# FFT convolution with two gated layers: the transform's last stores, fetches and a decoded weight piece in another order

## The chip, the cores and the metric

One core of a Trainium2 chip runs the whole program. The time is device time in microseconds (us), the median of three runs. Engines: TensorE (PE) multiplies matrices, VectorE (DVE), ScalarE (ACT) and GpSimd (POOL) work on elements, SyncE (SP) issues the transfers. DMA moves data between memory and the core.

## The reference

A circular convolution along the sequence by FFT, then two gated layers on 6016 tokens of 256 channels, all in float32:

```python
X = np.fft.rfft(x, axis=1)                      # x: 2 x 3008 x 256
Y = X * (filt_r + 1j * filt_i)[None, :, :]
x = np.fft.irfft(Y, n=3008, axis=1).reshape(6016, 256)
g = x @ w_gate                                  # 256 x 1536
x = (g / (1 + np.exp(-g)) * (x @ w_val)) @ w_out
h = x @ w_in                                    # 256 x 2048
return (h * np.clip(h + 3.0, 0.0, 6.0) / 6.0) @ w_out2
```

## The kernel before, in words

**Transform.** 3008 = 47 x 64, so the FFT is two stages of small matrix products. Sixteen steps k handle one slice of 32 channels of one batch each, batch 0 and 1 in turns of four, first the lower 128 channels (a = 0), then the upper (a = 1). A step's work is spread over the loop's turns: `over_n1(k)` (L415) and `over_n2(k)` (L431) on TensorE, `filter_product(k)` on VectorE (L444) and GpSimd (`us`, four operations), `back(k)` (L457) two turns later on TensorE, whose result ScalarE copies into `turned` (L462). `store` (L466) writes `turned` to memory, and a fetch (L526) reads it in another arrangement, since the last stage of the inverse needs the 47-part axis across partitions: `to_time` (L158) does that last stage for one block of up to 512 tokens. A batch has six blocks. Blocks 0 and 1 of batch 0 are made at the transform's end by `form`; all others inside the layers, fetched by `load_g` (L140).

**Precision.** Each operand is split in a high part (rounded, ScalarE: L116 for x, L486 and L487 for weights) and the low rest (VectorE or GpSimd subtracts: L109). `l1` makes a product of three: high by high, and each high by the other's low.

**Weights.** They come as 64-bit numbers and are decoded on the core, 128 columns of each matrix a piece f, by six steps on VectorE behind one on ScalarE: `start` (L187, ScalarE), `leading` = L196, L198, L201, `rest` = L204, L206, L112. Then come `high_w1` (ScalarE) and `low_w1` (VectorE or GpSimd). Two halves of a buffer (`x`) hold the pieces in turn, so piece f + 2 is loaded (`load_dec`, L479) when piece f is done with the half.

**Layers.** The first loop's turn t does one piece of one block: 12 matmuls L236 for gate and value, ScalarE's Silu (L613), VectorE's product (L622). The first 24 turns alternate between blocks 0 and 1, two turns each (p = t // 2), so that pieces are needed half as fast: f = 0 and 1 at t = 0 to 3, f = 2 at t = 4. After two turns of a block the hidden values are split into `hs` (ScalarE L116, VectorE L109), and after the following two turns of l1 TensorE takes them into the output product, 12 matmuls L121. This stage, where pieces are decoded beside the layers, runs to about 165 us.

**What sets the order.** Everything is written out by hand: each engine works its queue in the order in which the code emits. `at` and `send` put decode steps and transfers at turns k of the transform; `lead`, `rest` and `part` (L615) put `start` and `leading`, `rest`, and `high_w1` with `low_w1` at turns t of the layers. SyncE issues transfers in order, and a transfer that must wait holds up those behind it.

Of the kernel before, what the change touches and what calls it, by code (L numbers as in the profile page):

```python
# [9 lines left out]
F32 = mybir.dt.float32  # L10
# [6 lines left out]
P = 128  # L17
B, S, D = 2, 3008, 256
N1, N2 = 47, 64
N1P = 48  # L20
# [3 lines left out]
F1, F2 = DFF1 // P, DFF2 // P  # L24

BLOCKS = [(8 * j, min(8, N1 - 8 * j)) for j in range(6)]
# [52 lines left out]
def fft_conv_glu_mlp(ctx: ExitStack, tc: tile.TileContext, x, filt, mats, sgn, w1, w2, out):  # L79
    nc = tc.nc  # L80
# [4 lines left out]
    work = ctx.enter_context(tc.tile_pool(name="work", bufs=2))  # L85
# [39 lines left out]
    def rows(i, n=64):  # L125

        return slice(i * 64, i * 64 + n)

    def new_g():
        return work.tile([P, 7 * D], F32, tag="g", name="g", bufs=1)  # L130

    def turns(j, n):

        return 32 * j // N1, -(-(32 * j + n // 2) // N1)
# [9 lines left out]
    def new_xs():  # L144
        return work.tile([P, 2, 2, 512], F32R, tag="xs", name="xs")
# [85 lines left out]

    def l1(acc, w, xs, n):

        for r, v in ((0, 0), (0, 1), (1, 0)):
            for k in range(2):
                nc.tensor.matmul(acc[:, :n], w[:, r, k * P:(k + 1) * P], xs[:, v, k, :n],  # L236
                                 start=(r, v, k) == (0, 0, 0), stop=(r, k) == (1, 1))

    def l2(acc, w, hidden, first, last):
        hs, nt = hidden.hs, hidden.nt  # L240
# [72 lines left out]
    def new_y():  # L313
        return work.tile([P, 1024], F32, tag="y", name="y", bufs=1)
# [37 lines left out]
    with tc.manual_schedule():  # L352
# [10 lines left out]
        N = 16  # L363
# [132 lines left out]
        def at(k, step, *a):  # L496
            todo.setdefault(k, []).append(lambda: step(*a))

        def send(k, *a):
            moves.setdefault(k, []).append(a)  # L500

        moves = {}
        for k in range(1, 13):
            send(k, load_x, k + 3)
        for k, f in ((1, 0), (8, 1), (11, 2)):
            send(k, load_dec, f, 3)
        for j in range(4, 8):
            send(j - 2, load_filter, j)
        for i in range(8):
            send((5, 5, 6, 6, 7, 7, 8, 8)[i], store, 0, 0, i)  # L510
            send((9, 9, 10, 10, 11, 11, 12, 12)[i], store, 1, 0, i)
            send(13, store, 0, 1, i)

        for f, steps in ((0, (4, 5, 5, 6, 7, 8, 9, 10, 10)), (1, (10, 11, 11, 12, 12, 13, 14, 15, 17)), (2, (15, 15, 15, 17))):
            at(steps[0], lambda f: dec[f].start(), f)
            for i in range(len(steps[1:7])):
                at(steps[1 + i], lambda f, i: dec[f].part(i, nc.vector), f, i)
            if f < 2:
                at(steps[7], high_w1, f)
                at(steps[8], low_w1, f)  # L520

        def load_half(j, a, g):
            t0, t1 = turns(*BLOCKS[j][:1], BLOCKS[j][1] * N2)
            g = g[:, :7 * P].rearrange("p (t c) -> p t c", c=P)
            for r in range(2):
                nc.sync.dma_start(out=g[rows(r, N1P), :t1 - t0],  # L526
                                  in_=d2[0].rearrange("q (h n) c -> (q h) n c", h=2)[:, 32 * r + t0:32 * r + t1, a * P:(a + 1) * P])
            return g

        def form(j):  # L530
            xsd[j] = new_xs()
            acc = to_time(gt[j], j, "a")
            for r in range(2):
                split(*time_halves(xsd[j], acc, j, r))

# [3 lines left out]
        for k in range(N + 2):  # L539
            if 1 < k < N:  # L540
                over_n1(k)
            if k >= 2:
                back(k - 2)
            for step, *a in moves.get(k, ()):
                step(*a)
            if k == 12:
                g0 = new_g()
                gt[0] = [load_half(0, 0, g0)]
                gt[1] = [load_half(1, 0, new_y())]
            elif k == N - 1:  # L550
                gt[0].append(load_half(0, 1, g0[:, 7 * P:]))
                gt[1].append(load_half(1, 1, turned[:, 0].rearrange("p q c -> p (q c)")))
            if k < N:
                over_n2(k)
                filter_product(k)
            else:
                form(k - N)
            if k < 3 or 3 < k < 8:
                prepare_filter(k + (k < 3))
            for step in todo.get(k, ()):  # L560
                step()
        load_dec(3)

        n_pair = n_block * G1
        steps = [(s % 2, s // 2) for s in range(2 * G1)] + [divmod(s, G1) for s in range(2 * G1, n_pair)]
# [4 lines left out]
        for t in range(2 * n_pair):  # L572
            p, i = divmod(t, 2)
# [15 lines left out]
            if after:  # L589
                xsd[after] = new_xs()  # L590
                both_halves = to_time(gt[after], blocks[after][1])
            if i == 1 and p >= 1:
                kq, gq = steps[p - 1]
                if gq == 0:
                    accs[kq] = [bank("a") for _ in range(4 if kq > 1 else 2)]
                (l2 if kq > 1 else l2_plain)(accs[kq], wo1[:, gq], hid.pop(p - 1), gq == 0, gq == G1 - 1)
# [15 lines left out]
            h = hid[p].chunk(i)  # L612
            nc.scalar.activation(out=h, in_=hid[p].halves(gate), func=AF.Silu)  # L613

            lead, rest, part = ([f_ for f_ in range(2, F1) if t == 2 * f_ + d] for d in (-5, -4, -3))  # L615
            for f_ in part:
                high_w1(f_)
            for f_ in lead:
# [3 lines left out]
            nc.vector.tensor_tensor(out=h, in0=h, in1=hid[p].halves(val), op=ALU.mult)  # L622
            if i == 0 and p > plain:
                hid[p - 1].low()
            for f_ in part:
                low_w1(f_, nc.gpsimd)
                if f_ + 2 < F1:
                    load_dec(f_ + 2)
# [198 lines left out]
```

## Time and profile before

| | |
|---|---|
| median of 3 runs | 1187.62 us (1186.98 to 1189.38) |
| the profiled execution | 1187.92 us |
| its span, first to last instruction | 1186.1 us |
| TensorE clock granted (mean) | 0.998 |
| PE busy | 1167.2 us, 98% of the span |
| DVE busy | 1012.2 us, 85% |
| ACT busy | 612.8 us, 52% |
| POOL busy | 147.2 us, 12% |

TensorE fills nearly the whole span, so what counts is where it waits. The transform takes the first 78 us, and the places of interest lie between 60 and 170 us.

### The profile page before, as it was taken

To read this page: it belongs to the slowest core of one execution; us is meant where nothing else is said; L and a number is where in the kernel's file an instruction comes from. 1 tells how busy PE (TensorE), PEld (TensorE's weight loads), DVE (VectorE), ACT (ScalarE), POOL (GpSimd) and SP (SyncE) were. 2 spreads that over 40 slices of the span, in tenths; PEclk is the share of its full clock that TensorE was granted. 3 is DMA by queue.
4 is the path that set the end of the run, shared out by engine and by line. 5 is a ranking of instruction groups with operands and counts; after the bars stand their busy time and mean duration, and the time that the engine had idled before them with its cause. 6 is when DMAs were issued, how large, how long until landed. Compare 5 with 4: busy or idle time off the path is not lost.

```text
span 1186.1 us, 21856 instructions
## 1 busy us (share of the span) xinstructions
PE 1167.2 (98%) x9036; PEld 1022.9 (86%) x9036; DVE 1012.2 (85%) x1573; ACT 612.8 (52%) x928; POOL 147.2 (12%) x153
## 2 busy tenths in 40 slices
PE   9899999999999999999999999999999999999997
PEld 7677778888899888888889988998999999898997
DVE  5878896666678888778888899999999999999997
ACT  4553434433344444444445556666566666656654
POOL 4642310000002222022113300000000000000000
PEclk9999999999999999999999999999999999999999
DMA  8963501100113230221112201011001101100100
GB/s 292 290 168 102 147 1 57 24 20 24 31 54 87 83 94 34 87 60 54 39 32 99 80 16 36 1 37 36 18 18 36 34 1 36 36 17 20 34 19 17
DMA packets 43301, 70.33 MB, mean 59 GB/s; under 512 B 3712, under 2 KB 25088, under 8 KB 43200
## 3 DMA queue, kind: packets, MB, share of 16 engines
q1 hardware_dynamic: 42656, 68.40, 18.8%
q8 instruction: 71, 1.16, 0.4%
q10 hardware_dynamic: 544, 0.52, 0.1%
q14 instruction: 30, 0.25, 0.1%
HBM read 46.62 MB, written 22.28 MB: 58 GB/s over the span
## 4 chain that ended last, share of the span: by engine, by line
PE 95%; DVE 2%; DMA 1%; issue 1%; ACT 1%; SPq 0%; POOL 0%; ACTq 0%; DVEq 0%
PE gv L236 54%; PE a L245 32%; PE a L121 3%; PE gv L457 1%; PE gv L158 1%; PE a L431 1%; PE gv L415 1%; DVE hs L109 1%; DVE h L109 0%; DMA xin<-x_in 0%; DVE h L758 0%; SPq L466 0%; DMA d<-turned 0%; DMA g<-d 0%; PE a L158 0%
## 5 line engine op out<-in xcount | busy, mean ns | idle before, releaser
L245 PEld LDWEIGHTS a<-hs,wall 128*128 128x128 f32 x3276 | 408.3, 189 | 14.1 <-issue 1.2
L245 PE MATMUL a<-hs,wall 128*128 128x256 f32 (+1 forms) x3276 | 414.2, 282 | 1.8 <-issue 0.8
L236 PE MATMUL gv<-xs,wall 128*128 128x512 f32 (+1 forms) x1728 | 406.0, 390 | 0.0
L236 PEld LDWEIGHTS gv<-xs,wall 128*128 128x128 f32 x1728 | 320.8, 188 | 64.4
L109 DVE TENSOR_TENSOR hs<-h,hs 128x768 fp32r<-128x768 f32 (+2 forms) x324 | 349.5, 1079 | 21.9 <-ACT hs L292 16.8
L236 PE MATMUL gv<-xs,wi 128*128 128x512 f32 (+1 forms) x1152 | 276.0, 388 | 0.0
L236 PEld LDWEIGHTS gv<-xs,wi 128*128 128x128 f32 x1152 | 210.0, 188 | 37.1 <-DVE xs L109 0.4
L303 ACT CAST hs<-h 128x1024 fp32r<-128x1024 f32 (+1 forms) x156 | 160.8, 1031 | 114.6 <-DVE h L109 114.4
L292 ACT CAST hs<-h 128x768 fp32r<-128x768 f32 (+1 forms) x156 | 128.1, 821 | 151.0 <-PE a L245 102.4
L109 DVE TENSOR_TENSOR h<-h 128x512 f32<-128x512 f32 (+3 forms) x312 | 185.2, 593 | 6.8
L757 ACT ACTIVATE h<-gv 128x512 f32<-128x512 f32 (+1 forms) x192 | 110.0, 590 | 70.8 <-PE gv L236 54.0
L622 DVE TENSOR_TENSOR h<-h,gv 128x512 f32<-128x512 f32 (+1 forms) x144 | 96.7, 672 | 58.1 <-PE gv L236 56.8
L758 DVE SCALAR_TENSOR_TENSOR h<-h,gv 128x512 f32<-128x512 f32 (+1 forms) x192 | 128.7, 670 | 16.0 <-ACT h L757 11.1
L613 ACT ACTIVATE h<-gv 128x512 f32<-128x512 f32 (+1 forms) x144 | 84.8, 589 | 88.0 <-PE gv L236 87.6
L112 DVE TENSOR_TENSOR h<-h 128x256 f32<-128x256 f32 (+1 forms) x156 | 67.5, 432 | 2.1
L112 POOL TENSOR_TENSOR ww<-ww,wa 128x512 f32<-128x512 f32 x16 | 20.8, 1298 | 373.2 <-PE a L245 191.1
L121 PE MATMUL a<-hs,wall 128*128 128x512 f32 x144 | 36.5, 402 | 2.4 <-DVE hs L109 2.4
L121 PEld LDWEIGHTS a<-hs,wall 128*128 128x128 f32 x144 | 26.3, 188 | 12.2 <-DVE hs L109 6.8
L457 PE MATMUL gv<-us,mat 64*64 64x384 f32 x256 | 28.9, 490 | 3.5 <-issue 3.4
L109 POOL TENSOR_TENSOR wall<-x,wall 128x512 fp32r<-128x512 f32 (+1 forms) x20 | 22.9, 1168 | 68.5 <-ACT wall L486 68.5
L109 POOL TENSOR_TENSOR us<-us 128x192 f32<-128x192 f32 x32 | 25.9, 809 | 27.9 <-DVE us L444 23.0
L422 ACT COPY first<-gv 128x384 f32<-128x384 f32 x30 | 14.5, 482 | 26.0 <-PE gv L415 26.0
(83 smaller groups left out, 622.6 us busy)
## 6 DMA issues: line engine op xcount, KB each, us to landing
raw<-w_in SPq DMA_DIRECT2D x16, 512.0 KB, 4.4
xin<-x_in SPq DMA_DIRECT2D x30, 256.0 KB, 5.4
x<-w_in SPq DMA_DIRECT2D x9, 768.0 KB, 4.7
d<-turned SPq DMA_DIRECT2D x32, 192.0 KB, 5.0
yd<-y SPq DMA_DIRECT2D x10, 512.0 KB, 2.9
g<-yd SPq DMA_DIRECT2D x10, 512.0 KB, 3.8
y_out<-y SPq DMA_DIRECT2D x20, 256.0 KB, 2.4
wt<-wd SPq DMA_DIRECT2D x8, 448.0 KB, 3.4
```

What stands on the lines that cost most here:

```text
L109: (engine or nc.vector).tensor_tensor(out=out, in0=a, in1=b, op=ALU.subtract)
L112: (engine or nc.vector).tensor_tensor(out=out, in0=a, in1=b, op=ALU.add)
L121: nc.tensor.matmul(acc, w, v, start=first and i == 0, stop=last and i == 2)
L236: nc.tensor.matmul(acc[:, :n], w[:, r, k * P:(k + 1) * P], xs[:, v, k, :n], start=(r, v, k) == (0, 0, 0), stop=(r, k) == (1, 1))
L245: nc.tensor.matmul(acc[b][:, 256 * h:256 * h + nt], w[:, r, iw], hs[:, v, ih, :nt], start=first and h == 0 and v == 0 and r == 1, stop=las ...
L292: nc.scalar.copy(out=self.parts(0, 0, 3), in_=v(1, 4))
L303: nc.scalar.copy(out=self.parts(0, 3, 7), in_=self.values(4, 8))
L457: nc.tensor.matmul(accs[r][rows(h), :2 * COLS].rearrange("p (o n) -> p o n", o=2), mat[rows(r), w:w + N2], u[rows(r), :, part], start=m == ...
L613: nc.scalar.activation(out=h, in_=hid[p].halves(gate), func=AF.Silu)
L622: nc.vector.tensor_tensor(out=h, in0=h, in1=hid[p].halves(val), op=ALU.mult)
L757: nc.scalar.activation(out=h, in_=pre, func=AF.Relu, bias=3.0)
L758: nc.vector.scalar_tensor_tensor(out=h, in0=h, scalar=6.0, in1=pre, op0=ALU.min, op1=ALU.mult)
```

## The change

`l1` takes its three products in another order: high by high, then the weights' low part by x's high, then the weights' high by x's low. Blocks 0 and 1 are fetched in one piece for each half of the channels, instead of one for each block: `load_lower` at k = 11, `load_upper` at k = 13. The last stores of batch 0 are cut by rows instead of by frequencies: the first 11 rows of each of four groups of 32, which the two blocks read, go ahead of `load_upper`, and the other 21 behind it. Block 0 is formed at k = 16 as before; block 1's last inverse stage is emitted in the layers' turn t = 0 behind that turn's 12 matmuls, and its split behind that turn's product. Piece 2 is loaded at k = 14 (before: 11), and its decoding stands wholly in the layers: `start` and `leading` at t = 0, `rest` at t = 1, `high_w1` and `low_w1` at t = 2. Piece 1's steps stand one to a turn.

```diff
-        for r, v in ((0, 0), (0, 1), (1, 0)):
+        for r, v in ((0, 0), (1, 0), (0, 1)):
             for k in range(2):
                 nc.tensor.matmul(acc[:, :n], w[:, r, k * P:(k + 1) * P], xs[:, v, k, :n],
-                                 start=(r, v, k) == (0, 0, 0), stop=(r, k) == (1, 1))
+                                 start=(r, v, k) == (0, 0, 0), stop=(v, k) == (1, 1))
...
-        for k, f in ((1, 0), (8, 1), (11, 2)):
+        for k, f in ((1, 0), (8, 1), (14, 2)):
             send(k, load_dec, f, 3)
...
-            send(13, store, 0, 1, i)
-
-        for f, steps in ((0, (4, 5, 5, 6, 7, 8, 9, 10, 10)), (1, (10, 11, 11, 12, 12, 13, 14, 15, 17)), (2, (15, 15, 15, 17))):
+
+        for f, steps in ((0, (3, 4, 5, 6, 7, 8, 9, 10, 10)), (1, (10, 11, 12, 13, 14, 15, 16, 16, 17))):
             at(steps[0], lambda f: dec[f].start(), f)
-            for i in range(len(steps[1:7])):
+            for i in range(6):
                 at(steps[1 + i], lambda f, i: dec[f].part(i, nc.vector), f, i)
-            if f < 2:
-                at(steps[7], high_w1, f)
-                at(steps[8], low_w1, f)
-
-        def load_half(j, a, g):
-            t0, t1 = turns(*BLOCKS[j][:1], BLOCKS[j][1] * N2)
-            g = g[:, :7 * P].rearrange("p (t c) -> p t c", c=P)
+            at(steps[7], high_w1, f)
+            at(steps[8], low_w1, f)
+
+        t_end = turns(BLOCKS[1][0], BLOCKS[1][1] * N2)[1]
+
+        def load_lower():
+            g = new_g()[:, :t_end * P].rearrange("p (t c) -> p t c", c=P)
             for r in range(2):
-                nc.sync.dma_start(out=g[rows(r, N1P), :t1 - t0],
-                                  in_=d2[0].rearrange("q (h n) c -> (q h) n c", h=2)[:, 32 * r + t0:32 * r + t1, a * P:(a + 1) * P])
+                nc.sync.dma_start(out=g[rows(r, N1P)],
+                                  in_=d2[0].rearrange("q (h n) c -> (q h) n c", h=2)[:, 32 * r:32 * r + t_end, :P])
             return g
 
+        def store_rows(lo, hi):
+            for h in range(2):
+                for r in range(2):
+                    n = slice(64 * h + 32 * r + lo, 64 * h + 32 * r + hi)
+                    nc.sync.dma_start(out=d2[0][:, n, P:].rearrange("q p c -> p q c"), in_=turned[n, 0])
+
+        def load_upper():
+            g = work.tile([P, t_end * P], F32, tag="xs", name="upper").rearrange("p (t c) -> p t c", c=P)
...
         def form(j):
+            t0 = turns(BLOCKS[j][0], BLOCKS[j][1] * N2)[0]
+            acc = to_time([g[:, t0:] for g in halves], j, "a")
             xsd[j] = new_xs()
-            acc = to_time(gt[j], j, "a")
+            return acc
+
+        def form_end(j, acc):
             for r in range(2):
                 split(*time_halves(xsd[j], acc, j, r))
 
...
-            if k == 12:
-                g0 = new_g()
-                gt[0] = [load_half(0, 0, g0)]
-                gt[1] = [load_half(1, 0, new_y())]
-            elif k == N - 1:
-                gt[0].append(load_half(0, 1, g0[:, 7 * P:]))
-                gt[1].append(load_half(1, 1, turned[:, 0].rearrange("p q c -> p (q c)")))
+            if k == 11:
+                halves = [load_lower()]
+            elif k == 13:
+                store_rows(0, t_end)
+                halves.append(load_upper())
+                store_rows(t_end, 32)
             if k < N:
                 over_n2(k)
                 filter_product(k)
-            else:
-                form(k - N)
+            elif k == N:
+                form_end(0, form(0))
...
+            if t == 0:
+                acc1 = form(1)
...
-            lead, rest, part = ([f_ for f_ in range(2, F1) if t == 2 * f_ + d] for d in (-5, -4, -3))
+            lead, rest, part = ([f_ for f_ in range(2, F1) if t == max(2 * f_ - 5, 0) + d] for d in range(3))
...
+            if t == 0:
+                form_end(1, acc1)
```

TensorE's queue from the last `back` to the layers' first matmuls, before (L158 is block 1, its lower channels in `y`, its upper in `turned`; L236 the layers):

```order
L457 MATMUL gv<-us,mat 64x384 x8
L158 MATMUL a<-mat,y 64x26 x4
L158 MATMUL a<-mat,y 64x47 x16
L158 MATMUL a<-mat,y 64x42 x4
L158 MATMUL a<-mat,turned 64x26 x4
L158 MATMUL a<-mat,turned 64x47 x16
L158 MATMUL a<-mat,turned 64x42 x4
L236 MATMUL gv<-xs,wall 128x512 x48
```

And the same place in the change:

```order
L457 MATMUL gv<-us,mat 64x384 x8
L236 MATMUL gv<-xs,wall 128x512 x12
L158 MATMUL a<-mat,g 64x26 x4
L158 MATMUL a<-mat,g 64x47 x16
L158 MATMUL a<-mat,g 64x42 x4
L158 MATMUL a<-mat,upper 64x26 x4
L158 MATMUL a<-mat,upper 64x47 x16
L158 MATMUL a<-mat,upper 64x42 x4
L236 MATMUL gv<-xs,wall 128x512 x36
```

Block 1's 48 matmuls moved behind the layers' first twelve; `g` and `upper` are the new fetches.

VectorE's queue from the last filter product (L444) on, before (L109 `xs` splits blocks 0 and 1, two operations each; L109 `wall` is piece 1's low part; L112, L196 to L206 decode pieces 1 and 2 in `x`):

```order
L112 TENSOR_TENSOR x_101<-x_101 128x768
L444 TENSOR_TENSOR us<-a,side 128x384 x4
L196 TENSOR_SCALAR x_101<-x_101 128x768
L198 TENSOR_SCALAR x_101<-x_101 128x768
L109 TENSOR_TENSOR xs<-a,xs 128x2x256 x4
L109 TENSOR_TENSOR wall<-x_101,wall 128x512
L109 TENSOR_TENSOR wall<-x_101,wall 128x256
L201 SCALAR_TENSOR_TENSOR x_101<-x_101 128x768
L622 TENSOR_TENSOR h<-h,gv 128x512
```

And in the change, where L637 is the product that was L622:

```order
L444 TENSOR_TENSOR us<-a,side 128x384 x4
L206 SCALAR_TENSOR_TENSOR x_101<-x_101 128x768
L109 TENSOR_TENSOR xs<-a,xs 128x2x256 x2
L112 TENSOR_TENSOR x_101<-x_101 128x768
L109 TENSOR_TENSOR wall<-x_101,wall 128x512
L109 TENSOR_TENSOR wall<-x_101,wall 128x256
L637 TENSOR_TENSOR h<-h,gv 128x512
L109 TENSOR_TENSOR xs<-a,xs 128x2x256 x2
L196 TENSOR_SCALAR x_101<-x_101 128x768
L198 TENSOR_SCALAR x_101<-x_101 128x768
L201 SCALAR_TENSOR_TENSOR x_101<-x_101 128x768
L637 TENSOR_TENSOR h<-h,gv 128x512
```

Piece 1's last two steps moved behind the last filter product, and the leading steps of piece 2 moved behind the first product of the layers and block 1's split.

SyncE's queue at the transform's end, before (L466 and then L526 are batch 0's last stores and their fetch, L479 the loads of weight pieces):

```order
L526 DMA g<-d_0_72 48x6x128 x2
L526 DMA y<-d_0_72 48x6x128 x2
L466 DMA d_0_72<-turned 128x3x128 x8
L526 DMA g<-d_0_72 48x6x128 x2
L526 DMA turned<-d_0_72 48x6x128 x2
L479 DMA x_101<-w_in 128x1536 x2
```

And in the change:

```order
L533 DMA d_0_72<-turned 11x24x128 x4
L538 DMA upper<-d_0_72 48x11x128 x2
L533 DMA d_0_72<-turned 21x24x128 x4
L479 DMA x_101<-w_in 128x512 x3
L479 DMA x_101<-w_in 128x1536
```

The stores have 11 and 21 rows instead of 128, and piece 2's load (three parts) now stands behind all of them.

## Rows read from the trace of the kernel before

**Rows 1.** The page's head.
```profile
span 1186.1 us, 21856 instructions
```
**Rows 2.** Chain of waits, 58 to 100 us: start, length, what.
```profile
61.18 0.38 SPq L466
...
65.40 3.79 DMA d<-turned
...
69.72 3.50 DMA g<-d
...
75.39 1.59 PE a L158 x85
76.97 1.42 issue
```
**Rows 3.** Timeline of TensorE: start, length, line, tiles, count, idle before.
```profile
69.65 1.74 PE L457 MATMUL gv<-us,mat 64*64 64x384 f32 x14
...
78.58 11.40 PE L236 MATMUL gv<-xs,wall 128*128 128x512 f32 x48
90.51 3.05 PE L121 MATMUL a<-hs,wall 128*128 128x512 f32 x12 [0.53 <-DVE hs L109]
```
**Rows 4.** Timeline of VectorE.
```profile
74.80 1.29 DVE L109 TENSOR_TENSOR xs<-a,xs 128x512 fp32r<-128x512 f32 x2 [1.21 <-DMA turned<-d]
...
89.23 1.22 DVE L109 TENSOR_TENSOR hs<-h,hs 128x1024 fp32r<-128x1024 f32 x1
...
92.55 0.96 DVE L112 TENSOR_TENSOR x<-x 128x768 f32<-128x768 f32 x1
...
95.31 0.64 DVE L196 TENSOR_SCALAR x<-x 128x768 f32<-128x768 f32 x1 [1.21 <-ACT x L187]
96.06 0.91 DVE L198 TENSOR_SCALAR x<-x 128x768 uint32<-128x768 uint32 x1
97.00 0.96 DVE L201 SCALAR_TENSOR_TENSOR x<-x 128x768 uint32<-128x768 uint32 x1
97.88 1.22 DVE L109 TENSOR_TENSOR hs<-h,hs 128x1024 fp32r<-128x1024 f32 x1
99.02 0.68 DVE L622 TENSOR_TENSOR h<-h,gv 128x512 f32<-128x512 f32 x1
99.61 0.55 DVE L204 TENSOR_SCALAR x<-x 128x768 uint32<-128x768 uint32 x1
100.20 0.96 DVE L206 SCALAR_TENSOR_TENSOR x<-x 128x768 f32<-128x768 uint32 x1
101.19 0.96 DVE L112 TENSOR_TENSOR x<-x 128x768 f32<-128x768 f32 x1
```
**Rows 5.** Waits of TensorE's weight loads: us in total, times, longest.
```profile
PEld a L121 <- DVE hs L109: 6.8, 10, 2.3
```
**Rows 6.** Waits of VectorE from 66 to 172 us.
```profile
DVE x L196 <- ACT x L187: 10.8, 9, 1.2
```
**Rows 7.** Timeline of GpSimd.
```profile
68.28 1.31 POOL L109 TENSOR_TENSOR us<-us 128x192 f32<-128x192 f32 x1
69.55 0.59 POOL L112 TENSOR_TENSOR us<-us 128x192 f32<-128x192 f32 x1
...
72.27 0.90 POOL L109 TENSOR_TENSOR us<-us 128x192 f32<-128x192 f32 x1
...
94.24 2.32 POOL L109 TENSOR_TENSOR wall<-x,wall 128x512 fp32r<-128x512 f32 x2 [6.33 <-ACT wall L486]
```
**Rows 8.** Timeline of ScalarE.
```profile
74.18 1.07 ACT L116 CAST xs<-a 128x512 fp32r<-128x512 f32 x2 [1.58 <-PE a L158]
...
94.37 0.91 ACT L187 ACTIVATE x<-x 128x768 f32<-128x768 f32 x1
```
**Rows 9.** One window: busy time of PE, PEld, DVE, ACT, POOL, clock, DMA share, GB/s.
```profile
60.00:66.00 6.00, 5.65 (x142) 4.62 (x139) 5.17 (x9) 3.27 (x10) 5.34 (x7) 1.00 1.08 262
```
**Rows 10.** DMA issues from 30 to 95 us: count, size, median us to landing.
```profile
x<-w_in SPq DMA_DIRECT2D x6, 256.0 KB, 6.0
```

More of the change, by code (lines that the diff above doesn't have):

```diff
@@ new lines, in load_lower @@
+        def load_lower():
+            g = new_g()[:, :t_end * P].rearrange("p (t c) -> p t c", c=P)
+            for r in range(2):
+                nc.sync.dma_start(out=g[rows(r, N1P)],
+                                  in_=d2[0].rearrange("q (h n) c -> (q h) n c", h=2)[:, 32 * r:32 * r + t_end, :P])
+            return g
+        def store_rows(lo, hi):
[3 more added lines that the diff above has]
+                    nc.sync.dma_start(out=d2[0][:, n, P:].rearrange("q p c -> p q c"), in_=turned[n, 0])
@@ L528, in load_half @@
+        def load_upper():
+            g = work.tile([P, t_end * P], F32, tag="xs", name="upper").rearrange("p (t c) -> p t c", c=P)
+            for r in range(2):
+                nc.sync.dma_start(out=g[rows(r, N1P)],
+                                  in_=d2[0].rearrange("q (h n) c -> (q h) n c", h=2)[:, 32 * r:32 * r + t_end, P:])
             return g
         def form(j):
+            t0 = turns(BLOCKS[j][0], BLOCKS[j][1] * N2)[0]
+            acc = to_time([g[:, t0:] for g in halves], j, "a")
```

## The prediction

> **What bounds the kernel now.** I read the page first, then the chain of waits around the change, then the timelines of TensorE, VectorE, GpSimd and ScalarE there, then who waited for whom. The span is 1186.1 us [rows 1]; the profiled execution took 1187.92 us, so 1.82 us lie around the span, and the median of the runs shown (1187.62) is 0.3 us below it. My sums are made against 1187.92.
>
> The chain names the place that the change is about. The eight stores of batch 0's upper channels begin at 61.18 us, the last is issued at 65.40 and lands 3.79 us later, the fetch behind them takes another 3.50 us, and then come the inverse transforms of blocks 0 and 1 with a hole of 1.42 us on TensorE that the profile puts down to nothing [rows 2]. So the layers' first matmul starts at 78.58 us [rows 3].
>
> What follows it matters as much. After 48 layer matmuls (4 turns t of 12) TensorE starts the first output product at 90.51, 0.53 us late, and what it waited for is VectorE's `hs` [rows 3, 4]: 89.23 + 1.22 = 90.45. Over the whole stage the weight loads of that product waited 6.8 us for `hs`, 10 times [rows 5]. VectorE runs a closed ring there: the last step of one weight piece's decoding starts at 92.55 and of the next at 101.19 [rows 4], 8.64 us a piece. The only idle time in it is 1.2 us before L196, 9 times, 10.8 us in all [rows 6], and that wait is for ScalarE's L187, which itself stands behind two casts of the piece just decoded. No link of that ring is a TensorE result that is late. Hence in this stage TensorE's start is not what counts, but the moment at which VectorE ends its work for piece 3: L112 at 92.55 + 0.96 = 93.51 and `hs` at 90.45. Whatever moves these moves the stage's end, and from there the rest of the kernel, which TensorE fills.
>
> **The change, part by part.**
>
> *The fetch.* After, the wait on SyncE is for four stores of 11 rows (4 x 11 x 24 x 512 B = 0.54 MB) instead of eight of 192 KB (1.57 MB). They start at 61.18 as before, since ScalarE's copy that they read is not moved. From 61.18 to 65.40 the chain counts seven issues, 0.6 us each, so the fourth is issued at 63.0 and lands 3.8 us later, at 66.8 [rows 2]. Two fetches follow (0.54 MB, twice what the two that stood there before moved); with 3.50 us from issue to landing [rows 2] plus a second issue they are in by 71.2 to 72. TensorE ends `back(14)` at 69.65 + 1.74 = 71.4 [rows 3] and comes to the second half of block 0 some 0.9 us later, so I cost the fetch at nothing; it has cover until about 73.2, as the next paragraph shows.
>
> *TensorE to the first layer matmul.* Block 0 then runs without the hole for the fetch. A block's 48 matmuls are 96 records, at 1.59 / 85 us each [rows 2] 1.8 us, and the first of them fill `back(14)`'s gaps from 71.0 on: it ends at about 72.8. `back(15)` cannot come earlier than GpSimd's last filter product. Before, its third and fourth operations ran from 72.27 on, 0.90 us each [rows 7]. Now VectorE has piece 1's L206 (0.96 us alone) after that product in place of L196 and L198 of piece 2. Beside a VectorE operation with two tensor inputs GpSimd's third operation took 1.31 and the fourth started 1.27 later and took 0.59 [rows 7]: end 72.27 + 1.27 + 0.59 = 74.1. Eight of `back`'s matmuls are still to come, about 1.25 us: 75.4. The layers thus start at 75.4 instead of 78.58, 3.2 us earlier. Then 12 matmuls at 11.40 / 48 = 0.2375 us [rows 3] end at 78.2, and block 1's transform, now inside the layers, takes its 1.8 us: 80.0.
>
> *VectorE from there.* Block 1's casts take ScalarE 1.07 us for two [rows 8], the first 0.59, and VectorE's two subtractions 1.29 [rows 4]; the second ends at about 80.0 + 0.6 + 1.3 = 81.9. Everything of pieces 2 and 3 stands behind it on VectorE's queue. From the starts of the ring [rows 4], the pitch of each step is: L196 0.75, L198 0.94, L201 0.88, `hs` 1.14, the product with the gate (L622, now L637) 0.59, L204 0.59, L206 0.99, and L112 lasts 0.96. So from 81.9: piece 2's three leading steps to 84.5, product 85.1, its three others to 87.6; piece 3's leading steps to 90.2, `hs` until 91.4, product, L204, L206, and L112 ends at 81.9 + 2.57 + 0.59 + 2.54 + 2.57 + 1.14 + 0.59 + 0.59 + 0.99 + 0.96 = 94.4. Against 93.51 that is 0.9 us later, and `hs` with 91.4 against 90.45 likewise.
>
> Why later, when TensorE starts 3.2 us sooner? Before, L196 and L198 of piece 2 (about 1.7 us) ran while everything waited for the fetch; now they are in the crowded stretch, and VectorE has nothing to do while block 1 waits its turn behind 12 layer matmuls. It gets back one ring wait of 1.2 us, because piece 3's L187 no longer stands behind piece 2's casts. TensorE ends the four turns at 80.0 + 36 x 0.2375 = 88.6 and then waits for `hs` until 91.4.
>
> *Other edits, costed at nothing.* The order of l1's six matmuls asks for the low part of x two matmuls later and for the low part of the weights two earlier. Where x's low part is late it can win two matmuls, 0.5 us, but the first layer matmul now finds it ready. The weights' low part of pieces 2 and 3 comes from GpSimd, two operations in 2.32 us [rows 7] behind the casts, of which the first counts: before 92 and at about 96.5, asked for at 95 and 98. Spreading the steps of pieces 0 and 1 by one step each is covered by TensorE, busy for 5.65 of the 6 us from 60 to 66 [rows 9]. The smaller DMA load from 50 us on can only shorten the transform; its last steps wait on TensorE, so I take nothing, with a bound of 1 us of gain.
>
> *The one price that no row gives* is that of the stores of the remaining rows, four of 21 rows (1.03 MB), behind which piece 2's load now stands on SyncE's queue. All earlier transfers have 128 or 48 rows. At the 262 GB/s of 60 to 66 us [rows 9] the four take 3.9 us, from 69 to 73, and the load's three parts land at about 77.5: the last is issued when the first fetch is in, about 71.4, and such parts took 6.0 us from issue to landing [rows 10]. ScalarE comes to L187 at about 78.2, and nobody minds before 79.1 (80.0 less L187's 0.91 [rows 8]). This lower end, no cost, is the one I take, as its row is for stores of the same packets. The other end is rival 1.
>
> The sum: 1187.92 + 0.9 = **1188.8 us**.
>
> **The rule weighed against it.** The Trainium skill (DMA: Bandwidth & Descriptors, section Why a DMA increments its semaphore by 16 and not by 1) says that a transfer uses the largest number of engines up to 16 that divides the slowest dimension of both sides, so 11 rows run on 11 engines and 21 rows on 7; no run here has shown a transfer of such a count. By it the sum would be rival 1's; by the row's rate it stays as above.
>
> **The rivals.**
>
> 1. *Piece 2's load comes late.* If 21 rows are dealt whole to seven engines, three each, 1.03 MB go at 262 x 7 / 16 = 115 GB/s and take 9.0 us, until 78; the load's 0.79 MB behind them on the same engines takes 3.0 us more: 81. ScalarE stands at L187 from 78.2, and behind it in its queue are block 1's casts and the next Silu. L187 ends at 81.9, the casts at 83.0, VectorE's second subtraction at 83.8 instead of 81.9: 1.9 more, **1190.7 us**. It decides from a landing at 79.1 on, one for one. For it: 16 divides every earlier row count and not this one. Against it: fewer engines may each go faster than their share in a full stretch.
>
> 2. *TensorE decides after all.* If VectorE's steps pack closer than in the ring, the first output product moves with TensorE: 3.2 us sooner, 1.8 later for block 1, 0.5 less wait, **1186.0 us**. For it: 90.51 was only 0.53 late. Against it: VectorE's ring has no slack but ScalarE's 1.2 us.
>
> 3. *The fetch is still late*, so that the change doesn't do what it says. Two fetches of 270 KB, each behind four stores of few rows; if they land at 75.0 rather than before 73.2, all from `back(15)` on is 1.8 later: **1190.6 us**.
>
> **How the numbers follow.** My sum has 0.48, rival 1 0.32, rival 2 0.10, rival 3 0.07; 0.03 is left for something else. Within 0.2% (2.4 us, about what three runs spread over 2.4 us can tell) of 1187.62 lie nearly all of the first, most of rival 2 and a third of rival 1; slower are two thirds of rivals 1 and 3 and a little of the first; faster only the far side of rival 2 and a transform that gains its 1 us besides. That is 0.07, 0.60 and 0.33. The range runs from 1186.4 (part of rival 2) to 1191.5 (most of rivals 1 and 3); my sum's own is 1187.6 to 1190.0.
>
> **What would show it.** Right: the first L236 at about 75.4; no TensorE hole before it but the one for GpSimd; `hs` ending near 91.4 and the first L121 right behind, TensorE idle some 3 us before it; the next L112 8.64 us after the last. Rival 1: ScalarE idle before its first L187 in the layers, put down to the DMA of `x<-w_in`. Rival 2: the first L121 before 89.5. Rival 3: the second half of L158 on `upper` waiting for a DMA after 73. I would be wrong in kind if the transform before 69 us changed by more than 1 us, since I left it as it is.

## The result, and the profile after

The change made the kernel half a per cent slower: 1194.94 us median of 8 runs (1192.03 to 1196.84) against 1187.75 of 8 runs before (1186.76 to 1192.59), ratio 1.0053, 95% interval 1.004 to 1.0066. The forecast was 1188.8 us with a range up to 1191.5. The profiled execution took 1195.39 us; its span, 1193.5 us, is 7.4 us longer than before [rows 1].

The chain of waits of the changed kernel (start, length, what) answers to [rows 2]:

```profile
61.31 1.64 SPq L533
...
62.99 7.29 DMA d<-turned
...
70.34 3.97 DMA upper<-d
...
80.53 4.87 DMA x<-w_in
...
85.51 0.04 ACT x L187
```

The fourth store of 11 rows is issued at 62.99 and takes 7.29 us to land, where the last store of 128 rows took 3.79. The fetch behind it is in at 74.3. Then a new piece stands on the chain: the load of weight piece 2, which lands at 85.4.

SyncE's queue (issues; start, time from the first issue to the end of the last):

```profile
60.53 4.66 SPq L533 DMA_DIRECT2D d<-turned  x4
68.56 2.08 SPq L538 DMA_DIRECT2D upper<-d  x2
70.69 5.87 SPq L533 DMA_DIRECT2D d<-turned  x4
76.61 4.83 SPq L479 DMA_DIRECT2D x<-w_in  x4
```

The last two rows tell the rest: issuing four stores of 21 rows alone took 5.87 us, so the load behind them begins at 76.61 and its last part goes out after 80. ScalarE, TensorE and VectorE of the changed kernel, each from its timeline:

```profile
85.51 0.89 ACT L187 ACTIVATE x<-x 128x768 f32<-128x768 f32 x1 [5.02 <-DMA x<-w_in]
```
```profile
74.35 1.02 PE L158 MATMUL a<-mat,upper 48*64 48x47 f32 x43 [1.32 <-DMA upper<-d]
...
75.28 2.82 PE L457 MATMUL gv<-us,mat 64*64 64x384 f32 x15
78.04 3.14 PE L236 MATMUL gv<-xs,wall 128*128 128x512 f32 x12
...
82.65 3.04 PE L236 MATMUL gv<-xs,wall 128*128 128x512 f32 x12
87.41 5.86 PE L236 MATMUL gv<-xs,wall 128*128 128x512 f32 x24 [1.72 <-ACT xs L116]
98.02 4.92 PE L121 MATMUL a<-hs,wall 128*128 128x512 f32 x12 [4.75 <-DVE hs L109]
```
```profile
86.91 1.29 DVE L109 TENSOR_TENSOR xs<-a,xs 128x512 fp32r<-128x512 f32 x2 [4.94 <-ACT xs L116]
...
96.23 1.74 DVE L109 TENSOR_TENSOR hs<-h,hs 128x1024 fp32r<-128x1024 f32 x1
...
100.06 0.96 DVE L112 TENSOR_TENSOR x<-x 128x768 f32<-128x768 f32 x1
```

ScalarE stands 5.02 us at L187 for the load. Block 1's matmuls are done at 82.65, but its casts are queued behind L187, so VectorE's split ends at 86.91 + 1.29 = 88.20, and `hs` at 97.97 instead of 90.45 [rows 4]. Piece 3's L112 ends at 101.02 instead of 93.51: 7.5 us later, and the span ends 7.4 us later. From that L112 to the end both kernels take 1092.5 us (1193.5 - 101.02; 1186.1 - 93.51). So the whole loss is made before 101 us.

The profile of a single execution moves as a whole by a few us, because the transform takes more or less time. In what follows I therefore count from the end of the last filter product on VectorE (L444 `us`): 71.92 us before, 71.84 after.

### The profile page after: what moved, and what is told of

It is laid out like the page before. It is cut to its first block, busy times and chain, and to the rows that moved or that the text cites. A ratio compares the mean times of both kernels' runs of the same rounds, so it can differ in the third digit from the quotient of the medians.

```text
span 1193.5 us, 21852 instructions
## 1 busy us (share of the span) xinstructions
PE 1168.9 (98%) x9036; PEld 1026.1 (86%) x9036; DVE 1012.9 (85%) x1573; ACT 614.4 (51%) x928; POOL 146.8 (12%) x153
## 4 chain that ended last, share of the span: by engine, by line
PE 93%; DVE 3%; DMA 1%; issue 1%; ACT 1%; SPq 0%; POOL 0%; ACTq 0%; DVEq 0%
PE gv L236 53%; PE a L245 32%; PE a L121 3%; PE gv L457 1%; PE gv L415 1%; PE gv L158 1%; PE a L431 1%; DVE hs L109 1%; DMA d<-turned 1%; DVE h L109 0%; DMA x<-w_in 0%; DVE h L775 0%; DMA upper<-d 0%; PE gv L400 0%; DVE xs L109 0%
## 5 line engine op out<-in xcount | busy, mean ns | idle before, releaser
L236 PE MATMUL gv<-xs,wall 128*128 128x512 f32 (+1 forms) x1728 | 406.7, 390 | 1.7 <-ACT xs L116 1.7
L236 PEld LDWEIGHTS gv<-xs,wall 128*128 128x128 f32 x1728 | 320.6, 188 | 67.7 <-ACT xs L116 2.2
L109 DVE TENSOR_TENSOR hs<-h,hs 128x768 fp32r<-128x768 f32 (+2 forms) x324 | 350.5, 1082 | 22.0 <-ACT hs L292 16.9
L236 PE MATMUL gv<-xs,wi 128*128 128x512 f32 (+1 forms) x1152 | 275.8, 388 | 0.0
L236 PEld LDWEIGHTS gv<-xs,wi 128*128 128x128 f32 x1152 | 210.1, 188 | 36.8
L109 DVE TENSOR_TENSOR h<-h 128x512 f32<-128x512 f32 (+3 forms) x312 | 185.6, 595 | 6.8
L637 DVE TENSOR_TENSOR h<-h,gv 128x512 f32<-128x512 f32 (+1 forms) x144 | 96.9, 673 | 58.4 <-PE gv L236 57.1
L112 DVE TENSOR_TENSOR h<-h 128x256 f32<-128x256 f32 (+1 forms) x156 | 67.7, 434 | 2.1
L112 POOL TENSOR_TENSOR ww<-ww,wa 128x512 f32<-128x512 f32 x16 | 20.7, 1297 | 373.1 <-issue 190.8
L109 POOL TENSOR_TENSOR wall<-x,wall 128x512 fp32r<-128x512 f32 (+1 forms) x20 | 23.5, 1195 | 75.5 <-ACT wall L486 75.5
L457 PE MATMUL gv<-us,mat 64*64 64x384 f32 x256 | 29.0, 512 | 2.4 <-issue 2.3
L109 POOL TENSOR_TENSOR us<-us 128x192 f32<-128x192 f32 x32 | 25.5, 796 | 28.9 <-DVE us L444 26.7
```

The costliest lines, as they stand in the source:

```text
L109: (engine or nc.vector).tensor_tensor(out=out, in0=a, in1=b, op=ALU.subtract)
L112: (engine or nc.vector).tensor_tensor(out=out, in0=a, in1=b, op=ALU.add)
L457: nc.tensor.matmul(accs[r][rows(h), :2 * COLS].rearrange("p (o n) -> p o n", o=2), mat[rows(r), w:w + N2], u[rows(r), :, part], start=m == ...
```

## Experiments

| kernel | first L236 behind that product, us | `hs` end behind it, us | ratio to before, 95% |
|---|---|---|---|
| before | 6.66 | 18.53 | 1 |
| after | 6.20 | 26.13 | 1.0053 [1.004, 1.0066] |
| rows16 | 13.44 | 26.83 | 1.004 [1.0018, 1.0061] |
| rows16_step2 | 9.19 | 21.37 | 1.0012 [0.9997, 1.0027] |
| after_oldstores | 5.80 | 22.84 | 1.003 [1.0012, 1.0049] |
| after_load11 | 4.99 | 22.39 | 1.0042 [1.0023, 1.0061] |
| after_both | 7.50 | 24.85 | 1.005 [1.0036, 1.0064] |
| after_steps | 9.29 | 25.72 | 1.0054 [1.0036, 1.0072] |
| after_split | 3.68 | 20.04 | 1.0018 [1.0007, 1.003] |
| after_split_steps | 3.55 | 19.90 | 1.0019 [1.0, 1.0039] |
| l1_order | 6.36 | 18.25 | 0.9992 [0.9982, 1.0003] |
| start_first | 9.75 | 21.23 | 0.9971 [0.996, 0.9982] |
| block1_late | 3.86 | 16.40 | 0.9985 [0.9969, 1.0] |
| all_three | 3.83 | 16.91 | 0.9952 [0.9934, 0.9971] |

The columns of us are differences of starts and ends of rows in each profiled execution. Ratios and intervals come from all runs of a kernel and of before beside it, and can differ by some 0.1% from the quotient of the two medians. The medians of before beside the three groups were 1188.48, 1189.27 and 1187.91 us. My theory after the result: a store of few neighbouring rows is slow, which makes the fetch and then piece 2's load late. The rivals: the count of rows alone, or the load's place alone.

**rows16 and rows16_step2: is it the number of rows or which rows?** Both are the kernel before, its last eight stores cut by rows instead of by columns, 16 rows each; the one takes 16 neighbours, the other every second row.

```diff
-            send(13, store, 0, 1, i)
+            send(13, store_rows, i)
...
+        n = slice(16 * i, 16 * i + 16)                                  # rows16
+        n = slice(32 * (i // 2) + i % 2, 32 * (i // 2) + 32, 2)         # rows16_step2
+        nc.sync.dma_start(out=d2[0][:, n, P:].rearrange("q p c -> p q c"), in_=turned[n, 0])
```

> The kernel before, with batch 0's last eight stores cut by rows: each moves 16 neighbouring rows of 24 x 512 B, 196 KB as before, and the fetch waits for all eight as before. Theory A (what decides is how many groups of four neighbouring rows a store touches, about 25 GB/s a group: the changed kernel's 11 rows, three groups, ran at 68 to 90 GB/s and its 21 rows, five to six groups, at 130 to 150): four groups give about 100 GB/s, 1.57 MB take 15 us instead of 8, the layers start 6 to 7 us later, 1194 us. Theory B (what decides is into how many equal shares the row count divides): 16 divides evenly, no change, 1187.7 us.

> The same, but each store moves every second row of a group of 32, so 16 rows that touch all eight groups of four. Theory A: about 200 GB/s, 1.57 MB in 7.5 to 8 us, the layers start within 1 us of before, 1187.7 to 1188.7 us. Theory B: no change, 1187.7 us. If it were the cut by rows as such (24 short runs of each row), it would be as slow as with 16 neighbouring rows.

A window in which little but those stores moved, rows16 first (busy time of the engines, granted clock, the share of their time for which the 16 DMA engines were busy, GB/s):

```profile
66.00:68.00 2.00, 1.95 (x63) 1.18 (x59) 2.00 (x5) 1.12 (x4) 0.83 (x2) 1.00 0.73 122
```
```profile
66.00:68.00 2.00, 2.00 (x32) 0.96 (x28) 0.84 (x1) 0.89 (x3) 1.84 (x3) 1.00 1.01 184
```

The same number of rows, the same bytes, the same packets: 122 GB/s for neighbours, 184 for every second row (from 64 to 70 us 124 and 183). In rows16 TensorE then waits for the fetch:

```profile
77.79 0.45 PE L158 MATMUL a<-mat,g 48*64 48x47 f32 x2 [5.44 <-DMA g<-d]
...
85.35 12.92 PE L236 MATMUL gv<-xs,wall 128*128 128x512 f32 x48
```

The kernel is 0.4% slower with neighbours, and with every second row no different within what was measured, although its layers start 2.5 us later behind the last product and not within the 1 us that I expected. So at one count of rows the spread over the partitions decides. The changed kernel's own stores, 11 rows in the first stretch, 21 in the second:

```profile
62.00:68.00 6.00, 5.27 (x142) 4.47 (x143) 4.05 (x8) 2.97 (x9) 3.53 (x6) 1.00 0.58 76
74.00:80.00 6.00, 5.65 (x70) 3.73 (x71) 3.18 (x5) 2.77 (x7) 0.04 (x1) 0.72 0.50 141
```

These two were slow for different reasons, as the rows of the DMA queue tell (packets, MB, and the time that the packets took as a share of the 16 engines' time): first before from 62 to 68 us, 276 GB/s in all, where full-height stores run, then the two stretches.

```profile
q1 hardware_dynamic: 3339, 1.64, 100.8%
q1 hardware_dynamic: 855, 0.42, 56.2%
q1 hardware_dynamic: 1623, 0.83, 49.4%
```

Worked out from these, a packet took 29 ns before (1.008 x 16 x 6 us / 3339), 63 ns from 11 rows and 29 ns from 21. From 64 to 70 us the same sum gives 54 ns for rows16 and 43 for rows16_step2. So the packets of 11 rows were slow, as those of rows16 were. The packets of 21 rows were as fast as before's; they filled only half of the engines' time, so these stores lacked engines. No run kept the spread and changed the number of engines alone.

The Trainium skill (SBUF — State Buffer, section Door 1: The DMA port swizzle) says that a DMA is as fast as the SBUF ports that its partitions reach, four neighbours sharing one, at some 27 GB/s a port. By it my estimate is 11 / 4 x 27 = 75 GB/s for 11 neighbours, 143 for 21, 109 for 16, and 218 for every second row of 32. The trace agrees with 76 for 11. For 16 and for every second row it has the order, with 122 above the estimate and 184 below. The 141 for 21 agrees in number alone, since those packets were not slowed. The rule of the Trainium skill (DMA: Bandwidth & Descriptors, section Why a DMA increments its semaphore by 16 and not by 1) that the prediction weighed, by which 11 rows get 11 engines and 21 rows 7, would by itself make the 11 the faster; the measured order is the reverse. For the 21 rows the trace is near it: 7 of 16 engines are 44% of their time, and 49.4% was measured.

**after_load11, after_oldstores, after_both: the load, the stores, or both.** The changed kernel with piece 2's load sent at k = 11, ahead of all these stores; with before's eight column stores in place of the two groups; with both.

```diff
-        for k, f in ((1, 0), (8, 1), (14, 2)):
+        for k, f in ((1, 0), (8, 1), (11, 2)):          # after_load11, after_both
...
-                store_rows(0, t_end)
+                for i in range(8):                      # after_oldstores, after_both
+                    store(0, 1, i)
                 halves.append(load_upper())
-                store_rows(t_end, 32)
```

> The changed kernel with piece 2's load issued at k = 11 again, ahead of the row stores; stores and decoding as changed. If 5.0 us of ScalarE's wait at L187 are the main loss and the late fetch is the rest: L187 does not wait, block 1's split ends at about 84.5 us, L112 of piece 3 at 97 (before 93.5, changed 101.0), 1191 us. If the fetch alone decides, 1194 us; if L187's wait alone, 1188.5 us.

> The changed kernel with batch 0's last stores as they were (eight of 128 rows, all ahead of the fetch of the upper channels); all else as changed. If the row cut is what delays the fetch and, behind it, piece 2's load: the stores are in by 69, the fetch by 73, piece 2's load by about 77, ScalarE no longer waits at L187, and what is left is VectorE's later work: L112 of piece 3 ends 1 to 2 us after before's, 1189 to 1190 us. If the loss lies in the decoding moved into the layers: 1194 us, hardly better.

> The changed kernel with both the old stores and piece 2's load at k = 11: what is left is the joint fetch, block 1 inside the layers, piece 2's steps wholly in the layers, and l1's order. VectorE's work alone: the fetch lands at 73 as before, the layers start near 76, L112 of piece 3 ends 0.9 to 1.5 us later than before: 1188.5 to 1189.5 us. If TensorE's earlier start were what counts: 1186 us.

Either edit takes ScalarE's long wait away: `hs` comes at 22.4 and 22.8 us instead of 26.1. The times, 1193.02 and 1192.36 us, came down less than the 1191 and the 1189 to 1190 that I expected. And after_both, which has neither price, was expected near before and measured 1194.28 us, ratio 1.005, no better than the change. I had missed something. TensorE of after_both, and its clock (a window as above):

```profile
71.29 0.31 PE L158 MATMUL a<-mat,upper 48*64 48x47 f32 x2 [2.07 <-DMA upper<-d]
72.80 1.37 PE L158 MATMUL a<-mat,upper 48*64 48x47 f32 x43 [1.21 <-DMA upper<-d]
...
74.11 2.81 PE L457 MATMUL gv<-us,mat 64*64 64x384 f32 x15
76.85 4.05 PE L236 MATMUL gv<-xs,wall 128*128 128x512 f32 x12
```
```profile
74.00:78.00 4.00, 4.00 (x31) 2.21 (x26) 2.38 (x4) 1.95 (x5) 0.00 (x0) 0.50 0.05 18
```

TensorE stood idle for 2.07 and 1.21 us, and afterwards the granted clock was 0.50, the lower of its two levels (1.2 of 2.4 GHz), from 74 to 78 us. The 15 records of L457 took 2.81 us and the 12 layer matmuls 4.05. With eight old stores ahead of it the fetch is not earlier than before, and it is larger: block 0 waits for both blocks' rows, 2 x 264 KB, instead of its own 2 x 144 KB.

**after_steps, after_split, after_split_steps: what is left of after_both.** The first puts back the old steps of pieces 0 and 1, the second cuts the fetch so that block 0's rows (up to `t_first`) go first, the third does both.

```diff
-(0, (3, 4, 5, 6, 7, 8, 9, 10, 10)), (1, (10, 11, 12, 13, 14, 15, 16, 16, 17))    # after_steps, after_split_steps
+(0, (4, 5, 5, 6, 7, 8, 9, 10, 10)), (1, (10, 11, 11, 12, 12, 13, 14, 15, 17))
...
-                nc.sync.dma_start(out=g[rows(r, N1P)],                          # after_split, after_split_steps
-                                  in_=...[:, 32 * r:32 * r + t_end, P:])
+                nc.sync.dma_start(out=g[rows(r, N1P), :t_first],
+                                  in_=...[:, 32 * r:32 * r + t_first, P:])
+            for r in range(2):
+                nc.sync.dma_start(out=g[rows(r, N1P), t_first:],
+                                  in_=...[:, 32 * r + t_first:32 * r + t_end, P:])
```

> The kernel after_both with the old steps for pieces 0 and 1, so that piece 1's last VectorE step and ScalarE's casts of it stand ahead of block 0's xs split again. In after_both the first 12 gate and value matmuls took 4.05 us against 2.85, and VectorE's low part of piece 1 (wall, L109) came at 77.78, behind ScalarE's cast at 77.13. Theory (piece 1's late end is a price of its own): the first 12 take 2.8 to 2.9 us, and hs ends 1.1 to 1.2 us earlier after the last filter product (23.7 us behind it instead of 24.85); time 1.0 to 1.2 us under after_both, about 1193.0 against a before of 1189. Rival (the 12 are slow because of the half clock alone, 0.50 to 0.73 there): they still take 4 us, and the time stays at 1194.

> The kernel after_both with the upper half's fetch as four DMAs: block 0's six turns first (2 x 144 KB), then block 1's other five. In after_both block 0 waited for 2 x 264 KB, 5.4 us from the issue of the first to the last landing (67.34 to 72.76); in the kernel before block 0 waited for 2 x 144 KB, 3.9 us (69.35 to 73.22). Theory (the joint fetch is a price of its own): block 0's inverse stage has its second half 1.3 to 1.6 us earlier behind the issue, the first gate and value matmul stands 6.0 us behind the last filter product instead of 7.5, and the time is 1.3 to 1.6 us under after_both, about 1192.7 against a before of 1189. Rival (the stage waits for the whole tile, or the order of the queue makes no difference): 7.5 us and 1194.

> Both edits together on after_both. Theory (the two prices add up, and what is then left is piece 2's decode, all of it inside the layers and behind block 1's split on VectorE: 9.9 us from that split to hs against 6.9 in block1_late, which is this kernel with two of piece 2's steps ahead of the layers and a separate fetch): first 12 matmuls in 2.9 us, hs 22.2 us behind the last filter product, time 2.5 us under after_both, ratio to before 1.002 to 1.003. Rival (the loss of after_both is one thing that none of these edits touches, such as block 1's place or TensorE's clock): ratio 1.004 or more, with hs still 24 us or more behind the last filter product.

The steps are worth nothing that was measured: after_steps 1.0054, after_both 1.005. In its profile the first 12 layer matmuls took 3.12 us instead of 4.05, but came 1.8 us later behind the last product, after waits of 2.91 and 1.46 us for the fetch. My reason was wrong too, as t = 0 multiplies by piece 0 alone and cannot wait for piece 1. The cut of the fetch is worth 3.8 us between the two ratios (1.005 to 1.0018), over twice what I expected. TensorE of after_split, and the same window:

```profile
72.58 0.31 PE L158 MATMUL a<-mat,upper 48*64 48x47 f32 x2 [0.29 <-DMA upper<-d]
73.44 0.83 PE L158 MATMUL a<-mat,upper 48*64 48x47 f32 x43 [0.56 <-DMA upper<-d]
...
74.17 1.84 PE L457 MATMUL gv<-us,mat 64*64 64x384 f32 x15
75.93 3.05 PE L236 MATMUL gv<-xs,wall 128*128 128x512 f32 x12
```
```profile
74.00:78.00 4.00, 4.00 (x49) 2.65 (x40) 2.33 (x4) 1.90 (x4) 0.44 (x1) 1.00 0.64 201
```

The waits are 0.29 and 0.56 us, the clock stays at 1.00, and the same records take 0.83, 1.84 and 3.05 us instead of 1.37, 2.81 and 4.05: the wait is 2.4 us shorter, and another 2.5 us come back because TensorE is not slowed after it. That the clock fell because of the idle time is read from these two kernels side by side; no run changed the idle time alone. The length of one wait does not settle it either: after_split's TensorE waited 3.22 us for `hs`, the clock was 0.57 from 92 to 96 us, and the output product took 4.61 us; in after_both the same wait of 3.25 us left the clock at 1.00 from 94 to 98 us, and the product took 3.06. after_split_steps is the same within its interval, so 0.2% of the loss is left in both. It lies on VectorE, here in after_split:

```profile
81.21 1.29 DVE L109 TENSOR_TENSOR xs<-a,xs 128x512 fp32r<-128x512 f32 x2 [1.13 <-ACT xs L116]
82.42 0.55 DVE L196 TENSOR_SCALAR x<-x 128x768 f32<-128x768 f32 x1
...
90.55 1.74 DVE L109 TENSOR_TENSOR hs<-h,hs 128x1024 fp32r<-128x1024 f32 x1
```

From the end of the split (82.50) to that of `hs` (92.29) are 9.8 us, full of pieces 2 and 3.

**l1_order, block1_late, start_first, all_three: the rest of the change, and the ring.** All four stand on the kernel before. l1_order has the new order of l1's matmuls; block1_late has block 1's inverse stage behind the first 12 layer matmuls, but leaves piece 2's steps where they were and puts the split behind them (`form` is parted from `form_end` as in the change); start_first moves ScalarE's L187 ahead of the casts of the piece before; all_three has all of these edits.

```diff
-            for f_ in part:                             # start_first
-                high_w1(f_)
             for f_ in lead:
                 dec[f_].start()
+            for f_ in part:
+                high_w1(f_)
...
+            if t == 0:                                  # block1_late, behind l1
+                acc1 = form(1)
...
+            if t == 0:                                  # block1_late, behind dec[f_].leading()
+                form_end(1, acc1)
```

> The kernel before with l1's new order alone. Costed at nothing: 1187.7 us, within 0.5 us.

> The kernel before with block 1's last inverse stage behind the 12 layer matmuls of t = 0 and its split behind piece 2's last steps; stores, fetches, loads and the decode steps before the layers stay. By the ring: VectorE ends piece 2's L112 at about 81.6 instead of 84.9 and L112 of piece 3 at about 91 instead of 93.5, TensorE comes to the first output product at 88.6 instead of 90.5: 1185 to 1186 us. If moving block 1 behind the layers' matmuls is itself what hurts: 1188.5 us or more.

> The kernel before, where ScalarE does the next piece's L187 ahead of the two casts of the piece just decoded (two loops of four lines change places); no work is added or left out. If the closed ring VectorE L112, ScalarE's casts and L187, VectorE L196 paces the stage (8.64 us a piece, TensorE 8.38): VectorE's 1.2 us wait goes, the ring has 7.5 us, TensorE paces, nine pieces at 0.26 us and the 0.5 us at the first output product come back, 1185 us. If TensorE paces the stage already: no change, 1187.7 us.

> The kernel before with three edits that each ran alone: block 1's inverse stage and split behind t = 0's first matmuls (0.9985 alone), the start of a later piece ahead of the two casts on ScalarE (0.9971 alone), and the new order of l1's passes (0.9992 alone). Piece 2 keeps its steps ahead of the layers. Theory (hs and the ring of pieces start earlier by the one, each round of the ring's start by the other): the gains add up, ratio 0.994 to 0.996, 1182 to 1184 against a before of 1189. Rival (both gains are the same wait on VectorE's ring, so the second has nothing left to shorten): 0.997, as start_first alone.

l1_order makes no difference. In block1_late VectorE decodes the whole of piece 2 while it would wait for block 1's matmuls, and then needs 4.8 us from the split to `hs` (80.63 to 85.39) instead of after_split's 9.8:

```profile
78.47 0.96 DVE L112 TENSOR_TENSOR x<-x 128x768 f32<-128x768 f32 x1
79.35 1.28 DVE L109 TENSOR_TENSOR xs<-a,xs 128x512 fp32r<-128x512 f32 x2
...
84.17 1.22 DVE L109 TENSOR_TENSOR hs<-h,hs 128x1024 fp32r<-128x1024 f32 x1
```

(The 6.9 us in the expectation of after_split_steps was a slip of mine; the rows give 4.8.) block1_late's ratio, 0.9985, has 1 at the edge of its interval. start_first shortens the ring itself. In all_three the pieces follow each other by 8.2 us, 8.6 before [rows 4]:

```profile
91.21 0.96 DVE L112 TENSOR_TENSOR x<-x 128x768 f32<-128x768 f32 x1
...
99.44 0.96 DVE L112 TENSOR_TENSOR x<-x 128x768 f32<-128x768 f32 x1
```

The gains add up: 1182.65 us, ratio 0.9952, the fastest kernel of this study. From the last product to piece 3's L112 it takes 19.97 us (21.59 before), and from there to the end of the span 1089.2 (1092.6 before): 1.6 and 3.4, together 5.0 us, against 5.3 between the medians. In start_first's single profile the gain is smaller than its ratio says: there the fetch was issued only 0.4 us ahead of the end of the last product (2.6 before), and piece 3's L112 came 2.7 us later behind it; the ring then gave back 3.1.

## Why the prediction was wrong

*The fetch* is the step that failed, and in it one number. "The fourth is issued at 63.0" was right (62.99); "and lands 3.8 us later, at 66.8" was not: it took 7.29 us and landed at 70.3, since 11 neighbouring rows went at 76 GB/s, 63 ns a packet, and not at the 262 of full-height stores. The fetch was in at 74.3 instead of 71.2 to 72, past the 73.2 that I had named as its cover.

*The one price that no row gives* failed by the same assumption, that a store of few rows runs at the full rate. I had "the four take 3.9 us, from 69 to 73" at 262 GB/s; they began at 70.69, went at 141 GB/s and their issues alone held SyncE until 76.56. Rival 1 had the mechanism: fewer engines at work (it put the rate at 115 GB/s) and ScalarE at L187 in front of block 1's casts, with a landing at 81 and a price of 1.9 us. The load landed at 85.4; its last part went out only at 80.5. Rivals 1 and 3 were not alternatives: both hang on stores of few rows in one queue, rival 3 on their slow packets and rival 1 on the few engines, so both came together and on top of each other, which put the time above my range.

The 6.6 us by which `hs` (and, with 1195.39, the profiled execution) missed: block 1's matmuls ended at 82.65, and without the wait for the load its split would have ended 2.05 us later, as in after_both (82.37 to 84.42), at 84.7 instead of 81.9: 2.8 for the late fetch and the half clock after it. The load made it 88.20: 3.5 more. From the split to `hs` VectorE took 9.8 us instead of 9.5: 0.3. This splits one profile. after_both, without the slow stores and the late load, has `hs` 1.3 us nearer to the last product, and its time is no shorter by the intervals: its joint fetch is late behind the old stores too, and the clock falls.

*TensorE to the first layer matmul* was right where the fetch was in time: I had 3.5 us behind the last product, after_split has 3.68. From there to the end of block 1's split I had 6.5, after_split has 6.6. *VectorE from there* was right: 9.5 forecast, 9.8 in all seven kernels that have the change's decoding. So was the reading of the stage that the end follows VectorE's ring: rows16, with `hs` at 98.74 and a first layer matmul 6.8 us later than before, still takes 1092.6 us from piece 3's L112 to the end. after_split, the change without slow stores and with block 0's rows fetched by themselves, is 0.18% above before, 2.1 us (0.8 to 3.6), where my sum was 0.9.

One loss I saw and priced, the decoding of piece 2 that now stands behind block 1's split. What I did not see is that the clock takes part: a hole of 2 to 3 us before TensorE's last transform was costed by its length alone. *Other edits* were rightly costed at nothing: l1_order 0.9992 with 1 in its interval, the piece steps 1.0054 against 1.005, and in the two profiles the last filter product ended at 71.84 against 71.92, so no gain of the lighter DMA is seen.

Open remain 1.7 us that the profile puts down to VectorE's L112 in front of SyncE's L479 in the changed kernel; no run tells them from the stores' hold on the same queue. after_oldstores and after_both differ in the place of piece 2's load alone, and whether the early place costs anything (1.003 and 1.005, `hs` at 22.84 and 24.85) their overlapping intervals leave open. No run gave the 11-row stores the full rate, so what the change would bring with the stores that I forecast was not measured; after_split is the nearest. From 160 to 200 us the granted clock was 0.96 in after_both, after_load11, after_oldstores and block1_late and 1.00 in all the others, and these four spans are 1.1 to 1.6 us longer behind piece 3 than before's; why it fell there was not tried.

## What to carry to other kernels

Before a transfer is cut so that "only what is needed" goes first, look at which partitions the cut leaves, and at how many DMA engines are at work: a third of the bytes on 11 neighbouring rows took longer than all of them on 128 (9.8 us from the first issue to the last landing against 8.0), 21 rows kept about half of the engines busy, and whatever is queued behind pays as well. Price a smaller transfer by a row of the same height, and when two rivals hang on one unknown price, add them. And when a decoding step is moved, ask which idle time it was filling: the same work cost nothing while VectorE waited for block 1 and 5 us behind it.

## What the runs showed of the hardware

- Stores in packets of 512 bytes ran at 76 GB/s from 11 neighbouring partitions, 124 from 16 and 183 from 16 taken at every second partition, against 276 in before's stretch of 128; a packet took 63, 54, 43 and 29 ns.
- From 21 neighbouring partitions they ran at 141 GB/s, with 29 ns a packet, at 49% of the 16 engines' time (56% for the 11).
- SyncE's issues took longer for stores of few rows: 4.66 us for four of 11 rows, of which the first two took 0.35 and 0.34, and 5.87 us for four of 21, against 4.92 us for before's eight.
- Two waits of 2.07 and 1.21 us on TensorE were followed by a granted clock of 0.50 and cost 2.5 us beyond their length; waits of 0.29 and 0.56 us left it at 1.00. A single wait of 3.2 us was followed by a lower clock in after_split and not in after_both.
